# A two-stage convolution joint kernel: the second batch's first convolution as triples with running sums in one PSUM bank

## The chip, the cores and the metric

The kernel runs on one core of a Trainium2 chip. The metric is the device time of one launch in microseconds, the median of three runs. A core has five engines with queues of their own: TensorE (PE in the profile; it loads weights, PEld, and multiplies), VectorE (DVE), ScalarE (ACT), GpSimd (POOL) and SyncE (SP), which here only issues DMAs. TensorE writes its sums to PSUM, eight banks of 512 fp32 values in each of 128 partitions; VectorE and ScalarE read and write PSUM and SBUF, GpSimd SBUF alone.

## What is computed

```python
B, T, D, K, U = 2, 4000, 512, 5, 8       # x [B,T,D], w1, w2 [K,D,D], g [B,U,D], w_f, w_g, w_o [D,D], all bf16
xp = jnp.pad(x, ((0,0),(2,2),(0,0)))
h = sum(jnp.einsum("btc,cd->btd", xp[:, i:i+T, :], w1[i]) for i in range(K))
h = gelu(h)[:, ::2, :]                   # 2000 rows
hp = jnp.pad(h, ((0,0),(2,2),(0,0)))
f = sum(jnp.einsum("btc,cd->btd", hp[:, i:i+2000, :], w2[i]) for i in range(K))
f = gelu(f)[:, ::2, :]                   # 1000 rows: the features
fe = f @ w_f
ge = g @ w_g
j = jnp.tanh(fe[:, :, None, :] + ge[:, None, :, :])
return jnp.einsum("btud,dv->btuv", j, w_o)          # [2, 1000, 8, 512]
```

Two convolutions of five taps and stride two, each with a GELU, then a product with w_f, a tanh of its sum with each of 8 vectors, and a product with w_o for 16,000 rows.

## The kernel before

**Layout.** Channels lie on the 128 partitions, in four blocks (`NK`); time runs along the free dimension. The input is loaded by transposing DMAs, one for each phase of the row number, so that a stride becomes an offset. A "product" is one 512x128 weight matrix times one operand, for one block `m` of 128 outputs: four matmuls into one PSUM region.

**The first convolution, pairs from four phases.** `Tile_` makes outputs in pairs: from four phases of the input (rows modulo 4), with sums and differences of the phases and of the five weight matrices, two outputs cost 7 products where the plain way costs 10. `xf` (VectorE) makes the operands, `shift` (ScalarE) copies a phase moved by one. The first batch is cut into tiles of 252, 252 and 498 columns (tiles 0 to 2), the second into 504 and 498 (tiles 3 and 4). `unit(m)` runs the three products of the middle, a copy on ScalarE (`cs`), two VectorE sums back into PSUM, then (`end`) the four other products on top of these and a GELU to `hT`. `hT[b]` holds the result in six planes, by output number modulo 6.

**The second convolution, triples from six phases.** `Triple` makes three outputs with 9 products where the plain way costs 15. `HOME` says where each of the nine operands lies: in `row[b]` (place 0) or, in place, in `hT[b]` (place 1). `step` makes them: "2d" doubles three planes (two ScalarE copies, 1344 and 2688 values per partition), "r" takes their differences (VectorE, 4032), "prev" and "next" are copies of one plane on ScalarE, and nine further steps are VectorE operations of 1336. `unit(m)` uses three banks: t1 and s1 into b1, tm and sm into bm, t2 into b2; a ScalarE copy of b1; five VectorE operations of 334, two of which write back into PSUM; then t0 and s0 on top of b2, ti and si on top of bm. One output leaves from SBUF (`y`), two from PSUM, by GELU into `fT[b]` with a stride of three values (`o::3`). `w2part` makes the weight combinations.

**Features and outputs.** `fe(b)` multiplies the features by w_f; `ge` does g by w_g; `wosums` prepares sums of w_o on GpSimd in the place of w_g; `tanh(v, k)` on ScalarE writes a ring `jT`; `Plain` and `Seven` make the 125 output blocks of 128 rows, and `store` writes them to DRAM, with a cut wherever a block crosses from one of the 16 (batch, u) pairs to the next.

**Order.** The kernel is written as a list of operations. `Plan.edges` derives the dependences from SBUF bytes and PSUM banks, `Plan.schedule` fixes the order on each engine with a cost for each operation (0.16 us for a hand-over), and `emit` sets the semaphores. After line 823 the order on an engine isn't that of the list: TensorE, SP and GpSimd take the earliest entry of the list that is ready, ScalarE and VectorE the most urgent one. That order is fixed when the kernel is built; on the chip each engine goes strictly through its own.

**Names and lines of the change.** `load_x` (L417) with the calls in L441 to L442; `w2part` (L537); `Triple` (L639 to L732); `load_rest` (L839), which reloads `xs[0]` for the second batch and then loads w2 and the other weights; `tiles` and `trip` (L748 to L750); the tables `SUMS` and `LATE` (L897 to L904), which say after which unit each preparation is listed; the loops that follow; `store` (L957).

Of the kernel before, what the change touches and what calls it, by code (L numbers as in the profile page):

```python
# [12 lines left out]
P = 128  # L13
# [260 lines left out]
def bass_standalone__seq2seq_rnn_t_joint__speech_kernel(  # L274
# [36 lines left out]
    with ExitStack() as es:  # L311
# [22 lines left out]
        assert hT[0].end <= h_off + 16384 and xr[1].end <= cur[0]  # L334
        cs = [at(f"cs{i}", [NT], FP32) for i in range(2)]
# [10 lines left out]
        sd = [Buf(nc, f"sd{i}", [3, 336], FP32, s_off + i * 4096) for i in range(2)]  # L346
        assert sd[1].end <= ws[2].end
# [56 lines left out]
        for i in (0, 2):  # L404
            for ph in (2, 3):
                memset(xs[i][ph, :, 15:16])
# [17 lines left out]

        came = [load_xr(rt) for rt in range(2)]
# [15 lines left out]
        for ph in (2, 3, 1, 0):  # L441
            load_x(2, ph, 16, 528)  # L442
# [94 lines left out]
        def w2part(m, part):  # L537
# [7 lines left out]
            elif part == "p":  # L545
                stt("dve", w2_t[1, :, sl], w(2), 2.0, u)
                tt("dve", w(2), t, w(2), add)
            elif part == "a":
                act(w2_t[0, :, sl], v, ACT.Copy, scale=1.0 / 3.0)
                act(w(0), w(0), ACT.Copy, scale=0.5)  # L550
            else:
                sl = slice(m * P, (m + 2) * P)
                tt("dve", w2_t[2, :, sl], w2_sb[1, :, sl], w2_sb[3, :, sl], add)
                tt("dve", w2_t[3, :, sl], w2_sb[1, :, sl], w2_sb[3, :, sl], sub)
# [84 lines left out]
        class Triple:  # L639
# [5 lines left out]
            def __init__(self, b):  # L645
                self.b, self.z_, self.r_ = b, hT[b], row[b]

            def z(self, i, d=0, n=NT3):
                return self.z_[i, :, HOFF + d:HOFF + d + n]
# [4 lines left out]
            def step(self, which):  # L654
# [11 lines left out]
                elif which == "t2":  # L666
                    tt("dve", z(4), z(4), z(0), sub)
                elif which == "t1":
                    tt("dve", r(4), r(1), r(2), add)
                elif which == "tm":  # L670
                    tt("dve", r(5), r(2), r(1), sub)
                elif which == "ti":
                    tt("dve", r(3), r(1), r(3), sub)
                elif which == "t0":
                    tt("dve", r(0), r(0), r(2), sub)
                elif which == "s1":
                    tt("dve", z(0), z(1), z(3), add)
                elif which == "s0":
                    tt("dve", z(2), z(2), z(3), sub)
# [495 lines left out]
```

## Time and profile before

| | us |
|---|---|
| median of three runs (265.00 to 266.12) | 265.52 |
| the profiled execution | 265.86 |
| its span, first to last instruction | 264.1 |

The difference of some 1.8 us between the execution and its span lies around the span. The mean granted TensorE clock is 1.000.

Busy time by stage (us from the start of the span, busy us of each engine):

| stretch | what TensorE does | PE | DVE | ACT | POOL |
|---|---|---|---|---|---|
| 34.20 to 51.00 | first convolution, batch 0, tile 2 | 16.80 | 16.80 | 12.63 | 0.00 |
| 51.00 to 58.60 | tile 2 ends, tile 3 begins | 7.60 | 3.70 | 3.06 | 0.00 |
| 58.60 to 74.20 | tile 3 (batch 1) | 15.60 | 14.27 | 9.27 | 0.17 |
| 74.20 to 98.75 | tile 4 (batch 1) | 24.55 | 23.89 | 15.47 | 5.99 |
| 98.75 to 108.30 | tile 4 ends, second convolution begins | 9.55 | 4.44 | 3.22 | 0.00 |
| 108.30 to 131.60 | second convolution | 23.30 | 17.90 | 17.18 | 0.17 |
| 131.60 to 148.50 | features of batch 0, second convolution | 16.90 | 9.55 | 14.73 | 2.71 |
| 148.50 to 164.00 | second convolution ends, features of batch 1 | 15.35 | 7.38 | 11.66 | 11.04 |
| 164.00 to 264.00 | outputs | 96.10 | 85.72 | 89.28 | 58.74 |

A row of the timeline gives the start, the duration, engine, line, operation, output and input, shapes and count; rows of equal instructions are merged. The duration of one instruction reaches past the start of the next on the same engine, so what an instruction costs in a row of its kind is read from start to start. Nearly all operations are issued by helpers, so their line is that of the helper (L391 a matmul, L378 a tensor_tensor, L533 a scalar_tensor_tensor, L383 an activation) and the names of the operands tell them apart.

### The profile page before, as it was taken

The numbers are of one execution on the slowest core, as the hardware profiler recorded it, in microseconds if no ns is written. First come the engines' busy times: TensorE is split into PE (matmuls) and PEld (weight loads), VectorE is DVE, ScalarE is ACT, GpSimd is POOL, SyncE is SP. The second block draws the span as 40 slices with busy tenths as digits, with TensorE's granted clock in tenths as the row PEclk, the third lists the DMA queues.
The fourth block names the chain that finished last, engine by engine and source line by source line (L and its number), as shares of the span: only waits on it lengthen the run. The fifth ranks groups of instructions, "written<-read, shape, count | busy, mean of one in ns | idle before, by whom it ended". The sixth has DMA issues, their size and how long they took to land.

```text
span 264.1 us, 4770 instructions
## 1 busy us (share of the span) xinstructions
PE 257.3 (97%) x1738; PEld 167.3 (63%) x1738; DVE 209.9 (79%) x320; ACT 196.2 (74%) x269; POOL 80.1 (30%) x85
## 2 busy tenths in 40 slices
PE   8899999999999999999999999999999999999993
PEld 4797954444444445566646665777777777777782
DVE  1898999929999996299663744789899899889993
ACT  2637989348348723685679993898999999999942
POOL 1000000000000710000000974055785886929760
PEclk9999999999999999999999999999999999999999
DMA  6999999997000000000000000354454554645555
GB/s 246 301 178 196 201 211 217 191 352 224 2 0 0 0 2 0 0 2 1 0 2 0 20 24 0 126 167 159 155 185 142 170 180 139 207 144 171 168 181 172
DMA packets 54725, 31.92 MB, mean 121 GB/s; under 512 B 31646, under 2 KB 54446, under 8 KB 54702
## 3 DMA queue, kind: packets, MB, share of 16 engines
q1 hardware_dynamic: 54558, 31.55, 44.6%
q8 instruction: 14, 0.23, 0.4%
q14 instruction: 9, 0.07, 0.1%
q10 hardware_dynamic: 144, 0.07, 0.1%
HBM read 7.86 MB, written 16.38 MB: 92 GB/s over the span
## 4 chain that ended last, share of the span: by engine, by line
PE 88%; ACT 8%; DVE 1%; issue 1%; ACTq 0%
PE acc L391 88%; ACT jT L383 4%; ACT fT L383 2%; DVE xs L466 0%; ACT cs L383 0%; ACT xt L383 0%; ACT feT L383 0%; DVE xt L378 0%; DVE feT L872 0%; ACT og L383 0%; ACT hT L383 0%; PE acc L459 0%; ACTq L965 0%; ACT ost L383 0%; DVE zero L398 0%
## 5 line engine op out<-in xcount | busy, mean ns | idle before, releaser
L383 ACT ACTIVATE jT<-feT,geT 128x1000 bf16<-128x1000 f32 (+10 forms) x84 | 78.4, 1012 | 2.4 <-PE acc L391 1.4
L391 PE MATMUL acc<-wo_sb,jT 128*128 128x512 bf16 (+1 forms) x336 | 61.3, 323 | 0.0
L378 DVE TENSOR_TENSOR og<-acc,sn 128x512 bf16<-128x512 f32 x63 | 42.3, 684 | 9.9 <-ACT sn L383 7.4
L391 PE MATMUL acc<-xt,w_sb 128*128 128x252 bf16 (+2 forms) x240 | 45.9, 333 | 0.3 <-ACT hT L383 0.3
L378 POOL TENSOR_TENSOR ss<-jT 128x512 f16<-128x512 bf16 x21 | 24.4, 1164 | 71.5 <-PE acc L391 49.5
L391 PEld LDWEIGHTS acc<-wo_sb,jT 128*128 128x128 bf16 x336 | 32.9, 98 | 16.5
L383 ACT ACTIVATE sn<-acc 128x512 f32<-128x512 f32 x63 | 39.6, 677 | 4.3 <-PE acc L391 4.1
L391 PE MATMUL acc<-tw,ss 128*128 128x256 f16 x252 | 34.7, 273 | 0.0
L391 PEld LDWEIGHTS acc<-xt,w_sb 128*128 128x128 bf16 x240 | 23.3, 98 | 17.9 <-DVE ty L533 0.5
L955 DVE CAST ost<-acc 128x512 bf16<-128x512 f32 (+1 forms) x41 | 27.7, 676 | 2.4 <-PE acc L391 2.1
L391 PE MATMUL acc<-xs,w_t 128*128 128x498 bf16 (+2 forms) x140 | 29.5, 341 | 0.0
L391 PEld LDWEIGHTS acc<-tw,ss 128*128 128x128 f16 x252 | 24.6, 98 | 7.2
L383 ACT ACTIVATE hT<-acc 128x996 bf16<-128x996 f32 (+2 forms) x13 | 12.6, 968 | 21.0 <-PE acc L391 21.0
L378 POOL TENSOR_TENSOR ss<-jT,ss 128x512 f16<-128x512 bf16 x21 | 24.7, 1180 | 0.7
L378 POOL TENSOR_TENSOR ss<-ss,jT 128x512 f16<-128x512 f16 x21 | 24.5, 1169 | 0.7
L383 ACT ACTIVATE xt<-xs 128x1992 bf16<-128x1992 bf16 (+2 forms) x14 | 21.6, 1576 | 2.6 <-DMA xs<-in_x_dram 2.6
L391 PEld LDWEIGHTS acc<-xs,w_t 128*128 128x128 bf16 x140 | 13.5, 98 | 10.9 <-issue 0.3
L391 PE MATMUL acc<-xs,w_sb 128*128 128x252 bf16 (+2 forms) x104 | 19.3, 318 | 1.2 <-DVE xt L378 1.2
L378 DVE TENSOR_TENSOR ss<-jT 128x512 f16<-128x512 bf16 x21 | 16.7, 797 | 4.2 <-PE acc L391 2.2
L378 DVE TENSOR_TENSOR xt<-xt,xs 128x1992 bf16<-128x1992 bf16 (+2 forms) x14 | 14.2, 1012 | 5.7 <-ACT xt L383 5.7
L533 DVE SCALAR_TENSOR_TENSOR sd<-acc,cs 128x334 f32<-128x334 f32 x16 | 7.4, 499 | 12.9 <-PE acc L391 12.4
L391 PE MATMUL acc<-row,w_sb 128*128 128x334 bf16 x96 | 17.5, 305 | 0.0
(71 smaller groups left out, 363.3 us busy)
## 6 DMA issues: line engine op xcount, KB each, us to landing
out_dram<-og SPq DMA_DIRECT2D x75, 128.0 KB, 2.0
w_sb<-in_w_dram SPq DMA_DIRECT2D x10, 512.0 KB, 5.6
out_dram<-ost SPq DMA_DIRECT2D x34, 128.0 KB, 2.0
xr<-in_x_dram SPq DMA_DIRECT2D x2, 512.0 KB, 3.6
wg_sb<-in_w_g_dram SPq DMA_DIRECT2D x1, 512.0 KB, 8.8
wf_sb<-in_w_f_dram SPq DMA_DIRECT2D x1, 512.0 KB, 7.0
wo_sb<-in_w_o_dram SPq DMA_DIRECT2D x1, 512.0 KB, 7.9
xs<-in_x_dram SPq DMA_TRANSPOSE x16, 5.6
```

Of the source, the lines that this page charges most:

```text
L378: pl.op(eng, lambda e: e.tensor_tensor(out=o.ap, in0=a.ap, in1=b.ap, op=op), (a, b), (o,), 0.15 + 2.2e-3 * o.ap.free_size() if eng == "poo ...
L383: pl.op("act", lambda e: e.activation(o.ap, i.ap, func, scale=scale, bias=0.0 if bias is None else bias.ap), rd, (o,), o.ap.free_size() * ...
L391: ins = e.matmul(o.ap, lhsT=l.ap, rhs=r.ap, start=start and n == 0, stop=stop and n == len(pairs) - 1, skip_group_check=not check)
L533: pl.op(eng, lambda e: e.scalar_tensor_tensor(out=o.ap, in0=a.ap, scalar=f, in1=b.ap, op0=ALU.mult, op1=add), (a, b), (o,), vec_cost(o, (a ...
L955: pl.op("dve", lambda e: e.tensor_copy(out=o.ap, in_=v.ap), (v,), (o,), vec_cost(o, (v,)))
```

## The change

- **Input.** The second batch is loaded in six phases (rows modulo 6), 336 columns each, into `xp[2]` and, after the first batch's tile 1 is done, `xp[0]`, which lie in the place of `xs[2]` and `xs[0]`. For the last column of `xp[0]` four small DMAs load one row each, value by value.
- **First convolution of the second batch.** Tiles 3 and 4 go. Two `Triple`s (of 334 columns) take their place, with operands in `xp` and `row`, weights in `w1_sb`, `w1_t` and a new `w1_x`, and output to `hT[1]`.
- **Weights.** `w1part` makes w1's combinations while tile 2 runs, some in place in `w1_sb`, two of each block's sums on GpSimd. `w2part` scales some weights otherwise and moves the sum and difference of taps 1 and 3 to GpSimd, in blocks of 128. `w1_x` lies where w_f, w_g and w_o are kept, so these three are loaded later (`load_late`).
- **Units.** A unit of a triple uses one bank A for a running sum: t1 and s1, then ScalarE's copy `c`; tm and sm on top, then ScalarE's copy `s` (times -1.5); t2 on top, then two VectorE operations: `v` = A + s, and bank B = 2A + s. GpSimd adds `v` to `c`, from which one output leaves. t0 and s0 go on top of A, ti and si on top of B. The 16 units (two triples of the first convolution, two of the second, four blocks each, numbered 0 to 15) go through one loop in which three units overlap: s1 of t, s3 of t-1, s5 of t-2, s2 of t, s4 of t-1. `fixed` lists the preparation after each.
- **Features.** `fT` is written without a stride: outputs 0, 3, 6, ... first, then 1, 4, ..., then 2, 5, .... The rows of an output block are then three apart in DRAM, and `store` also cuts at the borders of these three planes (`R0`).

Kernel lines of the change, without the memory layout and the parts of `Triple.step` that are only rewritten:

```diff
+        xp = {i: Buf(nc, f"xp{i}", [6, NK, 352], BF16, xs[i].end - xs[i].bytes) for i in (0, 2)}
+        w1_x = Buf(nc, "w1_x", [3, NK, D], BF16, wf_sb.end - wf_sb.bytes)
...
+        def load_x6(i, b, ph, j0, col):
+            r0 = b * T + 6 * j0 + ph
+            dst = xp[i][ph, :, col:col + 336]
+            src = x.rearrange("b t d -> (b t) d")[r0:r0 + 6 * 335 + 1:6, :]
+            pl.dma("sp", lambda e: e.dma_start_transpose(out=dst.ap, in_=src), (), (dst,))
...
-        for ph in (2, 3, 1, 0):
-            load_x(2, ph, 16, 528)
+        for ph in (4, 0, 2, 1, 3, 5):
+            load_x6(2, 1, ph, 0, 16)
...
+                stt("dve", u, w(2), 2.0, u)
                 tt("dve", w(2), t, w(2), add)
-            elif part == "a":
                 act(w2_t[0, :, sl], v, ACT.Copy, scale=1.0 / 3.0)
-                act(w(0), w(0), ACT.Copy, scale=0.5)
+                act(w2_t[1, :, sl], u, ACT.Copy, scale=1.0 / 3.0)
             else:
-                sl = slice(m * P, (m + 2) * P)
-                tt("dve", w2_t[2, :, sl], w2_sb[1, :, sl], w2_sb[3, :, sl], add)
-                tt("dve", w2_t[3, :, sl], w2_sb[1, :, sl], w2_sb[3, :, sl], sub)
+                tt("pool", w2_t[2, :, sl], w(1), w(3), add)
+                tt("pool", w2_t[3, :, sl], w(1), w(3), sub)
+                act(w(1), w(1), ACT.Copy, scale=2.0)
+
+        def w1part(m, part):
+            sl = slice(m * P, (m + 1) * P)
+            w = lambda i: w1_sb[i, :, sl]
+            v, u = ssum[0][:], ssum[1][:]
+            if part == "s":
+                s = ws[m][:] if m < 2 else ws[2][:, (m - 2) * P:(m - 1) * P]
+                tt("dve", v, s, w(2), sub)
+                stt("dve", u, w(4), 4.0, w(0))
+                stt("dve", u, w(2), 2.0, u)
+                act(w1_x[0, :, sl], v, ACT.Copy, scale=1.0 / 3.0)
+                act(w1_x[1, :, sl], u, ACT.Copy, scale=1.0 / 3.0)
+                tt("pool", w(2), w(1), w(3), add)
+                tt("pool", w1_x[2, :, sl], w(1), w(3), sub)
+            else:
+                act(w(1), w(1), ACT.Copy, scale=2.0)
...
+            def s1(self):
+                self.A = banks.pop(0)
+                self.t.product("t1", self.m, self.A, True)
+                self.t.product("s1", self.m, self.A, False)
+                act(self.c, self.pa(), ACT.Copy)
+
+            def s2(self):
+                self.t.product("tm", self.m, self.A, False)
+                self.t.product("sm", self.m, self.A, False)
+                act(self.s, self.pa(), ACT.Copy, scale=-1.5)
+
+            def s3(self):
+                self.t.product("t2", self.m, self.A, False)
+                self.B = banks.pop(0)
+                tt("dve", self.v, self.pa(), self.s, add)
+                stt("dve", self.pb(), self.pa(), 2.0, self.s)
+                tt("pool", self.c, self.c, self.v, add)
+                self.t.out(1, self.m, self.c)
+
+            def s4(self):
+                self.t.product("t0", self.m, self.A, False)
+                self.t.product("s0", self.m, self.A, False)
+                self.t.out(0, self.m, self.pa())
+                banks.append(self.A)
+
+            def s5(self):
+                self.t.product("ti", self.m, self.B, False)
+                self.t.product("si", self.m, self.B, False)
+                self.t.out(2, self.m, self.pb())
+                banks.append(self.B)
...
+            for ph in (4, 0, 2, 1, 3, 5):
+                load_x6(0, 1, ph, 330, 0)
+            for ph in range(4):
+                d = xp[0][ph, :, 336:337]
+                pl.dma("sp", lambda e, d=d, ph=ph: e.dma_start(
+                    d.ap, x[1, T - 4 + ph:T - 3 + ph, :].rearrange("r (k p) -> p k r", p=P), allow_slow_non_contiguous=True), (), (d,), nbytes=65536)
             for i in (0, 1, 3, 4, 2):
                 load_w("sp", w2_sb[i], w2[i].rearrange("(k c) d -> c k d", c=P))
...
+        when(1, lambda: w1part(2, "d"), lambda: w1part(3, "d"), lambda: tail_zero(0))
+        steps(1, 1, 0, 4)
+        steps(2, 1, 4, 8)
+        steps(3, 1, 8, 13)
+        for m in range(NK):
+            when(1 + m, lambda m=m: w2part(m, "s"))
+            when(2 + m, lambda m=m: w2part(m, "d"))
+        steps(5, 2, 0, 4)
+        steps(6, 2, 4, 8)
+        steps(7, 2, 8, 13)
+        when(9, load_late, lambda: tail_zero(1))
+        steps(10, 3, 0, 4)
+        steps(11, 3, 4, 13)
+        when(12, ge)
+        when(13, lambda: fe(0))
+        when(14, lambda: tanh(0, 0), lambda: tanh(0, 1))
+        when(15, lambda: tanh(0, 2), lambda: tanh(0, 3))
+        nu = len(units)
+        for t in range(nu):
+            units[t].s1()
+            if t:
+                units[t - 1].s3()
+            if t > 1:
+                units[t - 2].s5()
+            else:
+                finish(1 - t)
+            units[t].s2()
+            if t:
+                units[t - 1].s4()
+            for f in fixed.get(t, ()):
+                f()
...
-                n = min((vv + 1) * T2, c0 + P) - lo
-                b, u, t = vv // U, vv % U, lo % T2
+                r = sum(lo % T2 >= q for q in R0[1:3])
+                n = min(vv * T2 + R0[r + 1], c0 + P) - lo
+                b, u, t = vv // U, vv % U, 3 * (lo % T2 - R0[r]) + r
                 s = src(lo - c0, lo - c0 + n)
-                dst = out[b, t:t + n, u, cl]
+                dst = out[b, t:t + 3 * n - 2:3, u, cl]
...
```

## The prediction

> **What bounds the kernel now.** I read the head of the page first, then what TensorE waits for, then its timeline for the price of a product, then VectorE's and GpSimd's timelines around the stages that change.
>
> The head of the page, and the rows of the span in 40 slices of 6.6 us:
> ```profile
> span 264.1 us, 4770 instructions
> PE 257.3 (97%) x1738; PEld 167.3 (63%) x1738; DVE 209.9 (79%) x320; ACT 196.2 (74%) x269; POOL 80.1 (30%) x85
> ...
> PE   8899999999999999999999999999999999999993
> ...
> DVE  1898999929999996299663744789899899889993
> ACT  2637989348348723685679993898999999999942
> POOL 1000000000000710000000974055785886929760
> ```
> PE is full in every slice between start and tail, at full granted clock. DVE is at 90% or more from slice 9 to 14 too (59 to 99 us), which is where the second batch's first convolution runs.
>
> All that TensorE waits for:
> ```profile
> PE acc L391 <- DVE zero L398: 1.2, 1, 1.2
> PE acc L391 <- DVE xt L378: 1.2, 1, 1.2
> PE acc L391 <- ACT hT L383: 0.3, 1, 0.3
> PE acc L391 <- DVE og L378: 0.2, 1, 0.2
> PE acc L391 <- ACT fT L383: 0.2, 1, 0.2
> ```
> 3.1 us in all, 2.4 of it before 9 us. So the time is the sum of matmul columns, and a product less is time gained as long as nobody else becomes late.
>
> TensorE's timeline, four matmuls (one product for one block of 128 outputs) to a row; the first number is the start:
> ```profile
> 68.80 1.01 PE L391 MATMUL acc<-xs,w_t 128*128 128x504 bf16 x4
> 69.64 1.01 PE L391 MATMUL acc<-xt,w_t 128*128 128x504 bf16 x4
> ...
> 86.99 1.00 PE L391 MATMUL acc<-xs,w_t 128*128 128x498 bf16 x4
> 87.83 1.00 PE L391 MATMUL acc<-xt,w_t 128*128 128x498 bf16 x4
> ...
> 98.75 0.73 PE L391 MATMUL acc<-row,w_sb 128*128 128x334 bf16 x4
> 99.31 0.73 PE L391 MATMUL acc<-hT,w_t 128*128 128x334 bf16 x4
> ```
> Durations overlap; the price is from start to start: 0.85 us for 504 columns (two such steps take 1.70), 0.84 for 498, 0.567 for 334 (98.75 to 100.45 is three).
>
> VectorE and then GpSimd around 90 us:
> ```profile
> 88.80 1.76 DVE L378 TENSOR_TENSOR hT<-hT 128x1336 bf16<-128x1336 bf16 x1
> 90.48 1.80 DVE L378 TENSOR_TENSOR row<-row 128x1336 bf16<-128x1336 bf16 x1
> ...
> 98.15 0.84 DVE L378 TENSOR_TENSOR hT<-hT 128x1336 bf16<-128x1336 bf16 x1
> 98.91 0.84 DVE L378 TENSOR_TENSOR row<-row 128x1336 bf16<-128x1336 bf16 x1
> ```
> ```profile
> 87.22 2.62 POOL L378 TENSOR_TENSOR tw<-wo_sb 128x512 f16<-128x512 bf16 x2 [24.45 <-PE acc L391]
> 89.80 3.49 POOL L378 TENSOR_TENSOR tw<-wo_sb,tw 128x512 f16<-128x512 bf16 x2
> ```
> The same step of a triple takes 0.76 us from start to start alone and 1.68 to 1.72 beside GpSimd. About 2.8 us were lost in three steps over 4.5 us of GpSimd (88.8 to 93.3): 0.63 us per us of overlap. The change puts GpSimd to work where it was idle, so this row matters most.
>
> **What it removes and adds on TensorE.** Removed: tiles 3 and 4, each 7 products x 4 blocks: 28 x 0.85 + 28 x 0.84 = 47.32 us. Added: two triples of 9 products x 4 blocks: 72 x 0.567 = 40.80. The second convolution keeps its 72 products, the features, sums and outputs their matmuls. Gain on the path: **6.52 us**, if TensorE stays full.
>
> **VectorE**, the cover that could break. Prices from start to start: first difference of a triple ("r") 2.18 us (85.45 to 87.63), its nine other steps 0.76 each, so 9.0 per triple; a weight sum of 512 0.60 (69.03 to 69.63); a sum on PSUM of 334 0.42, of 498 0.585 (two in 96.22 to 97.39). From 34.2 us (tile 2's first product) to unit 12's first (the second triple-batch of the second convolution) TensorE has 28 x 0.84 + 101 x 0.567 = 80.8 us: 12 units of nine products, less the seven of units 10 and 11 that come after it. In that time VectorE must do: what is left over from the tiles before (6.3, the rows from 34.6 to 42.5 that aren't tile 3's), tile 2's eight sums 4.7, four triples 36.1 less six steps that unit 12 needs later (4.6), w1's 12 weight sums 7.2, w2's 20 12.0, eleven units at two sums (five before) 9.2. Sum 70.9 of 80.8, so it fits with 10 us to spare.
>
> GpSimd alongside: 16 weight sums and 11 adds. A weight sum lies between 1.16 us (alone) and 1.74 (beside VectorE, the second pair above); I take 1.4. The fp32 add of 334 has no row; by elements it is 0.76 to 1.14, I take 0.95. Together 33 us, 41% of the stretch. VectorE's bf16 steps are the 36 us of triples; by chance 14.7 us of them lie beside GpSimd: 14.7 x 0.63 = 9.2 us. Bounds: 0 (all beside PSUM sums) and 33 x 0.63 = 20.8 (all beside steps). I take 9.2, as neither engine's order follows the other's: 80.1 of 80.8. VectorE thus goes from covered to just full.
>
> The Trainium skill ("GPSIMD Engine Reference", 1. Specifications) says more than the row: GpSimd shares its SBUF interfaces with VectorE, and every VectorE instruction with two SBUF inputs contends. The trace agrees for bf16 steps (1.68 against 0.76); no run here shows it for the weight sums, which also have two. By that rule 19.2 us more would be hit, 19.2 x 0.41 x 0.63 = 5.0 us, and VectorE would be 4.3 us over its stretch, for a time near 265.5.
>
> **ScalarE.** Per unit, two copies from PSUM of 334 (0.34 each, start to start, 0.45 long) and three GELUs (0.34 to 0.6); 6.0 us of copies per triple (3.55 for the pair of doublings, 81.77 to 85.32, then 1.2 twice); 24 weight scalings at 0.52 (86.68 to 87.20). With tile 2 and what is left before it 68 of 80.8 us, against 49.6 busy in that stretch now. It fits. Each unit adds two waits to TensorE: the next product into the same bank waits for ScalarE's snapshot. Behind the first lie three products of older units (1.70 us), behind the second four: a snapshot needs 0.45 plus about 0.1 of hand-over (0.02 to 0.14 in the chain of waits), so it is hidden. If it sits behind a 2.4 us doubling it costs 2.4 + 0.55 - 1.70 = 1.2 us; there are four such doublings, one per triple. The plan may run other units' products meanwhile.
>
> **Handovers.** Unit 12 needs hT[1] whole: unit 7's last product ends after 79 products, 57.7 + 44.8 = 102.5 us, GELU to 103.1, doublings 3.55, 0.5 of hand-over (the idle row before "r" says 0.62), "r" 2.18, three steps 2.3: 111.7, against a due time of 115.0. Three units' PSUM sums (2.5) and a unit of ScalarE (1.8) in between make it 116.0; all four VectorE pieces contended (4.5 more) 120.5, which is 5.5 late. TensorE has seven older products (4.0 us) to fill this. Units 4 and 8 have 3 to 4 us more room.
>
> **DMA.** Six transposes of 336 rows move what four of 512 did, at about 2.4 us per 512 KB one after the other. The one-column loads are 4 x 512 runs of two bytes; page section 3 gives 44.6% of 16 x 264 us over 54558 packets, 35 ns each, so 1.1 us per load on 16 engines, 4.5 together. They stand on SP ahead of w2, which then lands near 62 us; its sums can wait until 94. The last weights move behind unit 7's last use, three loads that land 7 to 9 us after issue, needed 12 us later. If this cover were gone, w2 late by x would be x on unit 8. On SP nothing stands behind the late loads until the first store at about 150. With w_o late, GpSimd's four sums of it (6.1 us, 87.2 to 93.3) move behind unit 12; their first product is at 155.26, so they stay hidden. I cost all at nothing. The split stores add about 32 issues at 0.45 us, 14 us, on SP, which waits for producers in every row of its list in the last 100 us: nothing. Contiguous feature writes make 24 GELUs shorter (0.74 towards 0.45 us), off the path where TensorE is full.
>
> **Sum.** Gain 6.52; loss between 0 and the 4.4 that handover and snapshots leave between them when some filler fails; I take the middle, 2.2. The profiled execution took 265.86 us: 265.86 - 6.52 + 2.2 = 261.5. The median is 0.34 lower: **261.2 us**; its own range, losses 0 to 4.2, is 259.0 to 263.2.
>
> **Rivals.**
> 1. *A late handover* (unit 12, with snapshots behind doublings). For: its chain has 3.3 us of slack alone, none contended. Against: the filler of 4.0 us, and 6.7 us of features that can run there. Without filler 5.5: 259.0 + 5.5 = 264.5 us.
> 2. *VectorE beside GpSimd becomes the bound.* Place: 34 to 115 us. Price 0.63 us per us of overlap. Without other loss it eats the gain when VectorE's work is 80.8 + 6.5 = 87.3, at 16.4 us of contention or 26 us of overlap out of 33; at all of it, 91.7, TensorE waits 10.9: 259.0 + 10.9 = 269.9 us. From 17.7 us of contention on it is slower beyond what can be told. For: the row, and adds that follow VectorE's sums at once, so they meet its next step. Against: half of VectorE's work is not bf16 steps.
> 3. *All hidden*: 259.0 us, a little less if the shorter GELUs help where the chain of waits runs through ScalarE (136 to 156 us).
>
> **Chances.** Forecast 0.56; late handover, 263.2 to 265.5, 0.17, half of it faster; contention, above 265.5, 0.24, 0.05 of it no change; all hidden and below 259.0, 0.03. A difference under 0.5% (1.33 us) can't be told from none here, so faster ends at 264.2 and slower begins at 266.85: 0.67, 0.14, 0.19. The range goes from 258.6 to 266.6 and leaves 0.2 out.
>
> **What would show it.** TensorE's 334-column products at 0.567 and 144 of them in triples; PE idle in 34 to 120 us of 0 to 4 us in all, its waits naming VectorE's hT or row at units 4, 8, 12; VectorE at over 95% busy there, with 1336-wide steps spread between 0.84 and 1.8; GpSimd about 33 us there. Wrong: over 5 us of PE waits on ScalarE's snapshots, or on a DMA; or VectorE with idle time while PE is full, so that contention was overrated.

## The result, and the profile after

The changed kernel takes **292.74 us** (median of four, 291.48 to 293.52) against 265.77 us in the same set of runs: a ratio of 1.101 [1.097, 1.106]. Predicted were 261.2 us and at most 266.6. The profiled execution took 292.66 us, its span 290.4, which is 26.3 us more than the 264.1 before. As the gain of 6.5 us was to come off, some 33 us were lost on the way.

The head of the page after, and the 40 slices, each now 7.3 us:
```profile
span 290.4 us, 5024 instructions
...
PE 259.2 (89%) x1788; PEld 172.9 (60%) x1802; DVE 215.2 (74%) x312; ACT 209.1 (72%) x319; POOL 124.6 (43%) x117
...
PE   8987999959985979899999999999978899985792
...
DVE  1999999953599999939622465787749798592982
...
POOL 1530200172476621121521794353953866298150
PEclk9999999996999799999999999999999999999999
```
Where TensorE was full in nearly every slice it now has holes in three places (slices counted from 0): shallow ones in slices 2 and 3, ahead of tile 2; deep ones between slices 8 and 14 (58 to 109 us), with reduced clock in slices 9 and 13, just after the deepest; and slices 29 to 37, in the outputs. GpSimd, which before did next to nothing until 86 us, works from slice 1 on.

All that TensorE waits for, the largest groups (us in total, times, longest):
```profile
PE acc L396 <- DVE acc L545: 6.7, 3, 3.3
PE acc L396 <- DVE og L383: 6.5, 6, 2.4
PE acc L396 <- DVE ost L1008: 3.3, 2, 2.7
PE acc L396 <- ACT sd L388: 2.7, 3, 1.7
PE acc L396 <- POOL w_sb L383: 1.7, 1, 1.7
PE acc L396 <- DVE w_t L383: 1.6, 3, 0.5
```
Three of these are in the units of the triples (`acc` written by VectorE, `sd` by ScalarE, `w_sb` by GpSimd), two in the outputs (`og`, `ost`), and `w_t` lies before tile 2, in the weights of the first batch.

Three marks divide the span, and they are used for every run below: tile 2's first product, the first product of the features of batch 1, and the end.

| us | before tile 2 | tile 2 to features of batch 1 | from there to the end |
|---|---|---|---|
| before | 34.2 | 122.2 | 107.7 |
| after | 37.9 | 132.8 | 119.7 |
| difference | +3.7 | +10.6 | +12.0 |

The middle should have become 6.5 us shorter, so 17.1 us are lost there. The last part, which the prediction costed at nothing, lost 12.0 us on its own.

### The profile page after: what moved, and what is told of

The parts are those of the page before. It is cut to its first block, busy times and chain, and to the rows that moved or that the text cites. A ratio compares the mean times of both kernels' runs of the same rounds, so it can differ in the third digit from the quotient of the medians.

```text
span 290.4 us, 5024 instructions
## 1 busy us (share of the span) xinstructions
PE 259.2 (89%) x1788; PEld 172.9 (60%) x1802; DVE 215.2 (74%) x312; ACT 209.1 (72%) x319; POOL 124.6 (43%) x117
## 4 chain that ended last, share of the span: by engine, by line
PE 49%; DVE 21%; DMA 8%; issue 6%; ACT 6%; SPq 5%; POOL 2%; ACTq 0%; DVEq 0%
PE acc L396 49%; DMA out_dram<-ost 8%; SPq L1019 5%; DVE row L383 4%; DVE xt L383 2%; DVE acc L545 2%; ACT jT L388 2%; POOL w_sb L383 2%; DVE xp L383 2%; DVE og L383 2%; DVE w_t L383 2%; ACT sn L388 1%; DVE ws L383 1%; DVE ws L545 1%; DVE ssum L383 1%
## 5 line engine op out<-in xcount | busy, mean ns | idle before, releaser
L396 PE MATMUL acc<-wo_sb,jT 128*128 128x256 bf16 (+1 forms) x322 | 60.1, 321 | 4.0 <-DVE ost L1008 3.3
L396 PEld LDWEIGHTS acc<-wo_sb,jT 128*128 128x128 bf16 x336 | 32.7, 98 | 20.1 <-DVE ost L1008 3.8
L383 POOL TENSOR_TENSOR sd<-sd 128x334 f32<-128x334 f32 x16 | 14.5, 905 | 58.3 <-DVE sd L383 51.4
L396 PE MATMUL acc<-row,w_sb 128*128 128x334 bf16 x160 | 29.4, 306 | 6.7 <-DVE acc L545 6.7
L396 PE MATMUL acc<-tw,ss 128*128 128x256 f16 x252 | 34.7, 273 | 0.0
L396 PE MATMUL acc<-xt,w_sb 128*128 128x252 bf16 (+1 forms) x144 | 25.1, 319 | 0.9 <-DVE xt L383 0.9
L396 PEld LDWEIGHTS acc<-row,w_sb 128*128 128x128 bf16 x160 | 15.1, 98 | 15.6 <-DVE acc L545 8.4
L383 POOL TENSOR_TENSOR w_sb<-w_sb 128x512 bf16<-128x512 bf16 x4 | 10.2, 2554 | 32.7 <-DVE ssum L545 19.5
L396 PE MATMUL acc<-xp,w_sb 128*128 128x334 bf16 x96 | 18.0, 312 | 1.7 <-POOL w_sb L383 1.7
L396 PE MATMUL acc<-tw,jT 128*128 128x256 f16 x84 | 12.7, 273 | 6.5 <-DVE og L383 6.5
L388 ACT ACTIVATE sd<-acc 128x334 f32<-128x334 f32 x32 | 14.3, 446 | 4.2 <-PE acc L396 4.1
L383 DVE TENSOR_TENSOR row<-row 128x1336 bf16<-128x1336 bf16 x16 | 16.9, 1054 | 0.0
```

The costliest lines, as they stand in the source:

```text
L383: pl.op(eng, lambda e: e.tensor_tensor(out=o.ap, in0=a.ap, in1=b.ap, op=op), (a, b), (o,), 0.15 + 2.2e-3 * o.ap.free_size() if eng == "poo ...
L388: pl.op("act", lambda e: e.activation(o.ap, i.ap, func, scale=scale, bias=0.0 if bias is None else bias.ap), rd, (o,), o.ap.free_size() * ...
L396: ins = e.matmul(o.ap, lhsT=l.ap, rhs=r.ap, start=start and n == 0, stop=stop and n == len(pairs) - 1, skip_group_check=not check)
```

## The experiments

All ratios are to the kernel before, run on the same chip in the same set.

### The outputs in the order of time again

The features get their old stride and the stores their old cuts; everything else stays as in the changed kernel.
```diff
-                act(fT[b][m, R0[r]:R0[r + 1]], src.map(lambda a: a[:, 0:n]), ACT.Gelu_apprx_tanh, scale=1.0 if r else 0.5)
+                act(fT[b][m, r::3], src.map(lambda a: a[:, 0:n]), ACT.Gelu_apprx_tanh, scale=1.0 if r else 0.5)
...
-                r = sum(lo % T2 >= q for q in R0[1:3])
-                n = min(vv * T2 + R0[r + 1], c0 + P) - lo
-                b, u, t = vv // U, vv % U, 3 * (lo % T2 - R0[r]) + r
+                n = min((vv + 1) * T2, c0 + P) - lo
+                b, u, t = vv // U, vv % U, lo % T2
...
-                dst = out[b, t:t + 3 * n - 2:3, u, cl]
+                dst = out[b, t:t + n, u, cl]
```


> The changed kernel with its features in time order again: GELUs write with a stride of three, a store is cut only where (batch, u) changes. From the features of batch 1 to the end the changed kernel took 119.7 us of its span, the one before 107.65. Theory: the stores of the planes cost these 12 us, so 280 to 282 us. Rival: the outputs are late because ScalarE and GpSimd reach them late; then the stores are a symptom and the time stays within 3 us of 292.7.

282.26 us, 1.061 [1.056, 1.065]: 10.5 us less than the changed kernel. The outputs take 108.0 us, as before the change. So the layout by planes costs the outputs their 12 us; the rest of the loss stands. The whole gains less than 12 us, as the middle becomes 1.8 us longer, 134.6 against 132.8; a GELU to `fT` takes 0.74 us there with the stride of three, and 0.46 without.

### That layout alone, in the kernel before

```diff
-                n = (T2 - o + 2) // 3
-                act(fT[self.b][m, o::3], src.map(lambda a: a[:, 0:n]), ACT.Gelu_apprx_tanh)
+                R0 = (0, 334, 667, 1000)
+                n = R0[o + 1] - R0[o]
+                act(fT[self.b][m, R0[o]:R0[o + 1]], src.map(lambda a: a[:, 0:n]), ACT.Gelu_apprx_tanh)
...
-                n = min((vv + 1) * T2, c0 + P) - lo
-                b, u, t = vv // U, vv % U, lo % T2
+                R0 = (0, 334, 667, 1000)
+                r = sum(lo % T2 >= q for q in R0[1:3])
+                n = min(vv * T2 + R0[r + 1], c0 + P) - lo
+                b, u, t = vv // U, vv % U, 3 * (lo % T2 - R0[r]) + r
...
-                dst = out[b, t:t + n, u, cl]
+                dst = out[b, t:t + 3 * n - 2:3, u, cl]
```


> The kernel before, with only the features by output plane and the stores that follow from it. Theory: the stores alone cost about 12 us, 276 to 279 us. Rival (outputs were late for another reason): 265 to 267 us, or a little under, since the 24 GELUs get shorter.

277.73 us, 1.047 [1.043, 1.051]; the outputs take 119.8 us. The layout does this without any triple in the first convolution. It consists of three things: contiguous features, rows three apart in DRAM, and cuts at 334 and 667. The next two runs take the cuts alone.

### The cuts alone, at 334 and 667, and at 336 and 672

Both keep the kernel before and the order of time, and only cut the stores more often.
```diff
-                n = min((vv + 1) * T2, c0 + P) - lo
+                R0 = (0, 334, 667, 1000)
+                n = min(vv * T2 + next(q for q in R0 if q > lo % T2), c0 + P) - lo
```


> The kernel before, features in time order, rows next to each other in DRAM, but every run of rows cut also at 334 and 667 of each 1000, as the planes cut it (172 stores in place of 140). Theory of the uneven cuts (odd row counts go to few DMA engines): nearly all of the 12 us, 275 to 279 us. Rival of the stride (rows three apart): 265 to 268 us. Theory of the issues: also 275 to 279, told apart by the next run.

```diff
-                n = min((vv + 1) * T2, c0 + P) - lo
+                R0 = (0, 336, 672, 1000)
+                n = min(vv * T2 + next(q for q in R0 if q > lo % T2), c0 + P) - lo
```


> As the run with cuts at 334 and 667, but cut at 336 and 672: about as many stores, every one a multiple of 8 rows. Theory of the uneven cuts: 265 to 268 us. Theory of the issues on SP: 274 to 279 us.

The cuts at 334 and 667, 172 stores: 278.15 us, 1.047 [1.044, 1.050]. The cuts at 336 and 672, 170 stores, each a multiple of 8 rows: 266.90 us, 1.003 [1.001, 1.005]. So the 30 further issues cost about 1 us. The other 11 us come with cuts that lie two to five rows elsewhere: the pieces then have uneven numbers of rows (61, 107, 109), where the even cuts leave multiples of 8. No cost of the rows three apart is seen: the plain cuts give the same time as the layout within the two intervals.

The stores of `og` in the trace. First SP's issues of them in the changed kernel (ns of one issue: least, median, most), and from issue to landing:
```profile
L1019 SPq DMA_DIRECT2D out_dram<-og x116: 255/401/3520, 180.3 to 286.8; - x116
...
DMA to landing us min/median/max: 1.7/3.7/6.8
```
The same of the kernel before with even cuts:
```profile
L966 SPq DMA_DIRECT2D out_dram<-og x114: 292/414/1426, 165.7 to 261.7; - x114
...
DMA to landing us min/median/max: 1.7/2.0/2.7
```
And of the kernel before with the cuts at 334 and 667:
```profile
L966 SPq DMA_DIRECT2D out_dram<-og x116: 260/393/3187, 165.9 to 275.2; - x116
...
DMA to landing us min/median/max: 1.9/3.4/6.7
```
The number of issues and their median are nearly the same in all three. What differs is how long a store takes to land (2.0 us against 3.4 to 3.7 in the median, up to 6.8), and that single issues stretch from 0.4 to over 3 us. The uncut kernel has 1.7/2.0/2.6. These landings are only those that the profile can assign: with the cuts at 334 and 667 they are 14 stores, all of them whole blocks of 128 rows. So the line shows that even a whole store lands late there, among the uneven ones; it does not show the uneven ones themselves.

A few pieces of the chain that ended last, in the changed kernel (start, us, what):
```profile
214.45 3.94 DMA out_dram<-ost
218.39 0.60 DVE ost L1008
...
220.71 3.74 DMA out_dram<-ost
...
225.10 3.80 DMA out_dram<-ost
```
A store must land before its buffer can be written again (`ost` by VectorE). Where a landing takes nearly 4 us, VectorE waits for the buffer, TensorE then for VectorE to empty PSUM: the 9.8 us of waits for `og` and `ost` above.

The Trainium skill ("DMA: Bandwidth & Descriptors", in the section on why a DMA increments its semaphore by 16) says that the queue takes for each transfer the largest number of engines up to 16 that divides the slowest dimension of both sides. An estimate by that rule: before the change all 140 stores go to 8 to 16 engines; with cuts at 334 and 667, 39 of the 172, with 2637 of the 16,000 rows, go to fewer than 8, and 12 of them to a single one. The trace agrees: on each of the 15 semaphores of the stores, before and after the change and with either set of cuts, the number of updates that come from the DMAs is what the rule gives, 16 for a store on 16 engines and one more than the rule's number for every other. With these numbers the updates of every block of 128 rows can be told apart. In the changed kernel the ten blocks with a piece on a single engine landed 6.5 us after their last issue in the median and 10.1 at most, and the 85 blocks wholly on 16 engines 4.3 us, against 2.0 before.

### The same stores, cut into multiples of 16 rows and a rest

The changed kernel with planes, where each run of rows is split so that its first part is a multiple of 16.
```diff
                 n = min(vv * T2 + R0[r + 1], c0 + P) - lo
+                n = n - n % 16 or n
```


> The changed kernel, planes kept, but every run of rows is cut into a multiple of 16 rows and a rest of under 16. Theory of the uneven cuts: a run of 37 or 67 rows can't be shared out over many DMA engines, so with cuts at 16 most of the 12 us come back, 281 to 285 us. Rival of the stride: rows that lie three apart in DRAM are slow, whatever the cut, 291 to 294. Rival of the issues: SP issues too many stores; some 40 more make it 295 or more.

293.58 us, 1.105 [1.100, 1.109]: no better. The landings are short again (1.7, 1.8 and at most 3.8 us), but there are 242 stores instead of 172, and at 0.42 us each they take 100 us of SP's time in outputs of 122 us. TensorE still waits 6.7 us for VectorE's `og`. It looks as if one fault had been exchanged for another, but that the issues on SP are the limit here was not tested; the fault of uneven rows is shown by the pair of runs before this, not by this one.

### The 16 weight sums on VectorE instead of GpSimd

In the changed kernel, with planes:
```diff
-                tt("pool", w2_t[2, :, sl], w(1), w(3), add)
-                tt("pool", w2_t[3, :, sl], w(1), w(3), sub)
+                tt("dve", w2_t[2, :, sl], w(1), w(3), add)
+                tt("dve", w2_t[3, :, sl], w(1), w(3), sub)
...
-                tt("pool", w(2), w(1), w(3), add)
-                tt("pool", w1_x[2, :, sl], w(1), w(3), sub)
+                tt("dve", w(2), w(1), w(3), add)
+                tt("dve", w1_x[2, :, sl], w(1), w(3), sub)
```


> The changed kernel with the 16 sums and differences of taps 1 and 3 of both weights on VectorE, not on GpSimd; the 16 adds of units stay there. Theory: they cost VectorE more from GpSimd (31.4 us of GpSimd, each VectorE operation beside it about 1 us longer) than on itself (16 x 0.35 = 5.6 us); the 3.7 us lost before tile 2 come back and most of the 17 us of waits between tile 2 and the features of batch 1, so 272 to 280 us. Rival: VectorE was full already, the sums push it over; 293 to 298 us.

276.99 us, 1.043 [1.039, 1.047]: 15.7 us less than the changed kernel, although VectorE gets 16 instructions more. They take 0.33 us each there from start to start where nothing hinders them, 5.3 us for 16, and are busy for 7.5 us in the trace; on GpSimd the same sums took 31.4 us. The marks are 34.7 and 154.5, so start and middle gain 3.2 and 13.0 us.

What the sums did on GpSimd is seen from 85 to 99 us in the changed kernel. VectorE's timeline there:
```profile
85.98 1.80 DVE L383 TENSOR_TENSOR row<-row 128x1336 bf16<-128x1336 bf16 x1
87.70 1.80 DVE L383 TENSOR_TENSOR xp<-xp 128x1336 bf16<-128x1336 bf16 x1
...
91.15 0.84 DVE L383 TENSOR_TENSOR xp<-xp 128x1336 bf16<-128x1336 bf16 x1
...
94.61 1.64 DVE L545 SCALAR_TENSOR_TENSOR ws<-w_sb 128x512 f32<-128x512 bf16 x1
96.17 1.64 DVE L383 TENSOR_TENSOR ssum<-ssum,w_sb 128x512 f32<-128x512 f32 x1
```
GpSimd's, three sums to a row:
```profile
85.30 5.21 POOL L383 TENSOR_TENSOR w_t<-w_sb 128x512 bf16<-128x512 bf16 x3
...
94.10 4.72 POOL L383 TENSOR_TENSOR w_t<-w_sb 128x512 bf16<-128x512 bf16 x3
```
And TensorE's:
```profile
89.56 0.74 PE L396 MATMUL acc<-xp,w_x 128*128 128x334 bf16 x4
93.65 0.74 PE L396 MATMUL acc<-row,w_sb 128*128 128x334 bf16 x4 [3.35 <-DVE acc L545]
94.23 0.73 PE L396 MATMUL acc<-xp,w_sb 128*128 128x334 bf16 x4
94.79 1.20 PE L396 MATMUL acc<-row,w_t 128*128 128x334 bf16 x4
95.79 1.32 PE L396 MATMUL acc<-xp,w_sb 128*128 128x334 bf16 x4
```
Beside GpSimd (85.3 to 90.5) a step of a triple takes 1.72 us from start to start, alone (91.15) 0.76; and a weight sum of 512, 0.60 us alone, takes 1.56. So the weight sums are slowed as the steps are. VectorE has no idle time here; its units' sums on PSUM come after the steps, and TensorE waits 3.35 us for them.

The Trainium skill ("GPSIMD Engine Reference", 1. Specifications) says that every VectorE instruction with two inputs from SBUF contends with GpSimd. The weight sums at 1.56 against 0.60 us show it here.

The loss is not only VectorE's pace. Around 60 us the chain goes through four engines. In the changed kernel GpSimd, then ScalarE, then VectorE:
```profile
56.93 6.90 POOL L383 TENSOR_TENSOR w_sb<-w_sb 128x512 bf16<-128x512 bf16 x2 [18.91 <-DVE ssum L545]
```
```profile
62.76 0.63 ACT L388 ACTIVATE w_sb<-w_sb 128x512 bf16<-128x512 bf16 x1 [5.24 <-POOL w_sb L383]
```
```profile
64.83 0.69 DVE L383 TENSOR_TENSOR ssum<-ws,w_sb 128x512 f32<-128x512 f32 x1 [3.11 <-ACT w_x L388]
```
The first row is two sums; the second of them, and VectorE's steps beside the first:
```profile
62.69 1.15 POOL L383 TENSOR_TENSOR w_sb<-w_sb 128x512 bf16<-128x512 bf16 x1
```
```profile
56.78 0.84 DVE L383 TENSOR_TENSOR xp<-xp 128x1336 bf16<-128x1336 bf16 x1
57.54 0.84 DVE L383 TENSOR_TENSOR row<-row 128x1336 bf16<-128x1336 bf16 x1
```
So the first sum took 5.8 us (56.93 to 62.7) and the second 1.15. VectorE's steps beside the first kept their usual 0.76 us: here GpSimd bore the whole contention. Behind the first sum stands a scaling in ScalarE's fixed order (5.24 us idle), behind that the scalings that free `ssum` for VectorE (3.11 us idle), and TensorE waits 1.7 us for the sum and 1.7 for ScalarE's snapshot.

### Sums on GpSimd in the kernel before

Of the change, only w2's sums of taps 1 and 3 move to GpSimd, in blocks of 128 (eight instructions of 512 instead of four of 1024 on VectorE).
```diff
-                sl = slice(m * P, (m + 2) * P)
-                tt("dve", w2_t[2, :, sl], w2_sb[1, :, sl], w2_sb[3, :, sl], add)
-                tt("dve", w2_t[3, :, sl], w2_sb[1, :, sl], w2_sb[3, :, sl], sub)
+                for i in (m, m + 1):
+                    sl = slice(i * P, (i + 1) * P)
+                    tt("pool", w2_t[2, :, sl], w2_sb[1, :, sl], w2_sb[3, :, sl], add)
+                    tt("pool", w2_t[3, :, sl], w2_sb[1, :, sl], w2_sb[3, :, sl], sub)
```


> The kernel before, with one part of the change alone: the sum and the difference of w2's taps 1 and 3 on GpSimd, eight operations of 512 in place of four of 1024 on VectorE. Theory: VectorE is full from 59 to 99 us; it saves 4 x 0.60 = 2.4 us and loses about 1 us beside each GpSimd sum, 8 in all, so TensorE waits 2 to 6 us, 268 to 272 us. Rival: VectorE gains 2.4 us and the time stays at 265 to 266.5.

269.56 us, 1.014 [1.011, 1.016]: 3.4 us slower, though VectorE has less to do. Six of the sums took 9.9 us, 1.65 each. The prediction's rate of 0.63 us lost per us of overlap would make that 6.2 us of VectorE's time. TensorE, full before, shows one wait of 2.94 us that ends at 89.2 us, and half a clock after it for 1.7 us more; its middle is 4.8 us longer than before (127.0 against 122.2). The wait is for ScalarE's GELU to `hT`, which stands behind two doublings (84.6 to 88.2 us) and these behind a scaling that waited 1.7 us for VectorE's `ssum`. So the loss came as a late link in ScalarE's order, 15 us after the last of the moved sums. The orders on the engines moved with the edit, so not all of the 3.4 us is shown to be contention.

### Time order and sums on VectorE together

The changed kernel with the first edit above and the sums' one, whose cores are:
```diff
-                act(fT[b][m, R0[r]:R0[r + 1]], src.map(lambda a: a[:, 0:n]), ACT.Gelu_apprx_tanh, scale=1.0 if r else 0.5)
+                act(fT[b][m, r::3], src.map(lambda a: a[:, 0:n]), ACT.Gelu_apprx_tanh, scale=1.0 if r else 0.5)
...
-                tt("pool", w(2), w(1), w(3), add)
+                tt("dve", w(2), w(1), w(3), add)
...
```

> The changed kernel with both undone: features in time order, and the 16 weight sums on VectorE. If the two losses add up, 292.7 - 10.5 - 15.7 = 266.5; but the trace of dve_sums reaches the features of batch 1 at 154.5 us, 1.9 us ahead of the kernel before, and the outputs in time order took 108 us, so 262 to 265 us. A rival says that ScalarE, with strided GELUs again, becomes the bound: 267 to 270.

265.97 us, 0.9995 [0.998, 1.001]. The two costs lie in different stages and add up: 10.5 and 15.7 singly make 26.2, and together the two edits bring 26.8. The expectation of 262 to 265 had counted on the features of batch 1 at 154.5 us, as in the run before with contiguous writes; with the stride they come at 156.4. The kernel now stands where it stood before the change; the gain of 6.5 is still covered by something.

### The units' adds on VectorE too

On top of the last kernel, GpSimd's last part in the triples: the add of `v` to `c`, 16 instructions of 334.
```diff
-                tt("pool", self.c, self.c, self.v, add)
+                tt("dve", self.c, self.c, self.v, add)
```


> As order_dve, and the 16 adds of units on VectorE too, so that GpSimd has no sum in this stretch. Each add on GpSimd makes VectorE's next step 0.5 us longer (1.36 for 0.84 in dve_sums); on VectorE it costs 0.42. Theory: no dearer for VectorE and a hand-over less before the GELU, 0 to 2 us less than order_dve. Rival: VectorE's own 6.7 us more make it late, 1 to 4 us more than order_dve.

261.76 us, 0.984 [0.982, 0.986]: 4.2 us less, where 0 to 2 were expected. Windows of 20 us (start and end; length; busy us and instructions of PE, PEld, DVE, ACT, POOL; granted clock; DMA), with the adds on GpSimd:
```profile
75.00:95.00 20.00, 19.14 (x134) 12.75 (x133) 20.00 (x28) 13.47 (x27) 3.06 (x4) 1.00 0.00 1
95.00:115.00 20.00, 18.23 (x125) 11.52 (x124) 18.31 (x31) 14.13 (x26) 3.68 (x5) 1.00 0.26 80
```
and on VectorE:
```profile
75.00:95.00 20.00, 20.00 (x143) 13.72 (x142) 20.00 (x34) 13.65 (x28) 0.00 (x0) 1.00 0.00 1
95.00:115.00 20.00, 19.86 (x141) 13.41 (x140) 20.00 (x37) 16.36 (x29) 0.17 (x1) 1.00 0.25 80
```
In the first 20 us VectorE is full in both and does 28 instructions with GpSimd beside it, 34 without. Each add meets the step that follows the unit's sums, as these rows show, GpSimd's and VectorE's, of the run with planes, the sums on VectorE and the adds on GpSimd (step 1.28 us from start to start instead of 0.76):
```profile
74.04 0.89 POOL L383 TENSOR_TENSOR sd<-sd 128x334 f32<-128x334 f32 x1 [6.13 <-DVE sd L383]
```
```profile
74.28 1.36 DVE L383 TENSOR_TENSOR xp<-xp 128x1336 bf16<-128x1336 bf16 x1
75.56 0.84 DVE L383 TENSOR_TENSOR row<-row 128x1336 bf16<-128x1336 bf16 x1
```
The 0.5 us that an add costs VectorE is more than the 0.4 that it takes on VectorE, but 0.1 us for each of 16 adds is 1.6 us at most. TensorE's waits for `sd`, `acc` and `fT` fall from 3.8 to 0.9 us, which is most of the 4.2; that they fall because the unit's own chain has a hand-over less is argued, not shown.

### w1's weight work held back until tile 2

In the changed kernel, four of w1's sums are put on GpSimd at 10.4 us, among the first batch's weights: they were the earliest entries ready in the plan. Here every operation of `w1part` depends on tile 2's first product.
```diff
         def w1part(m, part):
+            first = len(pl.ops)
+            w1part_(m, part)
+            for o in pl.ops[first:]:
+                o.after.append(gate[0])
...
+        gate.append(len(pl.ops))
```


> The changed kernel with w1's weight work (on ScalarE, VectorE and GpSimd) held back until tile 2's first product. Theory: the four GpSimd sums at 10.4 to 16.7 us made VectorE's steps of tile 0 late, so tile 2 begins at 34 to 35 us in place of 37.9; the sums are still due later, where VectorE is full, so of these 3 us between 0 and 3 stay: 289.5 to 293. Rival: tile 2 begins late for another reason (loads, order), and its start stays at 37 to 38.

291.61 us, 1.096 [1.093, 1.099]: 1.1 us less, which the two intervals do not tell apart. What VectorE did at the start, in the kernel before and in the changed one:
```profile
11.26 1.22 DVE L378 TENSOR_TENSOR w_t<-w_sb 128x2048 bf16<-128x2048 bf16 x1
```
```profile
13.53 2.17 DVE L383 TENSOR_TENSOR w_t<-w_sb 128x2048 bf16<-128x2048 bf16 x1
```
Held back, the first stretch is 34.0 us long instead of 37.9, so the early weight work is what made it late; with the sums on VectorE it was 34.7, so nearly all of it was the sums on GpSimd. But the middle grows from 132.8 to 134.9 us, TensorE's waits for VectorE's `acc` from 6.7 to 8.7 and its wait for GpSimd's `w_sb` from 1.7 to 3.0: the sums now collide there.

### All three edits and the hold

The kernel of the adds (time order, sums and adds on VectorE) with the hold of `w1part`:
```diff
-                tt("pool", self.c, self.c, self.v, add)
+                tt("dve", self.c, self.c, self.v, add)
...
+            for o in pl.ops[first:]:
+                o.after.append(gate[0])
...
```

> As order_dve_adds (features in time order, weight sums and adds on VectorE), with w1's weight work held back until tile 2's first product. There TensorE waited 1.3 us for VectorE at 23.8 us, behind four early weight sums at 12.8, and tile 2 began at 35.2 (34.2 in the kernel before). Theory: 0.5 to 1.3 us less, 260.4 to 261.3. Rival: the work is missed later, 262 to 264.

**260.40 us**, 0.979 [0.977, 0.981]: the fastest, and the change's triples are all in it. The page's rows:
```profile
span 258.0 us, 4983 instructions
...
PE 251.3 (97%) x1802; PEld 173.1 (67%) x1802; DVE 216.5 (84%) x344; ACT 210.8 (82%) x319; POOL 79.5 (31%) x85
...
PE   8999999999999999999999899999999999999993
```
and its waits:
```profile
PE acc L396 <- DVE zero L403: 1.2, 1, 1.2
PE acc L396 <- ACT sd L388: 0.7, 1, 0.7
```
Parts of the span: 33.3, 117.1 and 107.6 us, against 34.2, 122.2 and 107.7 before. The median gains 5.8 of the 6.5 us. The middle, where the triples are, gains 5.1; the 0.9 us at the start lie within what the start varies by (33.25 to 34.2 in the kernel before and its variants).

### The largest doubling in two

The same, with "2d"'s copy of 2688 values split into two of 1344, since TensorE's wait for `sd` is for a snapshot queued behind it.
```diff
-                    act(r(slice(1, 3), n=E), z(slice(0, 4, 2), 0, E), ACT.Copy, scale=2.0)
+                    act(r(1, n=E), z(0, 0, E), ACT.Copy, scale=2.0)
+                    act(r(2, n=E), z(2, 0, E), ACT.Copy, scale=2.0)
```


> As best_gate, with the 2688-wide doubling on ScalarE cut into two of 1344, so that a snapshot waits behind 1.3 us and not 2.4. Snapshots behind a doubling cost TensorE 1.15 us once in dve_sums. Theory: 0 to 0.7 us less than best_gate. Rival: a fixed cost of 0.1 us for each of four more copies, no difference.

260.72 us, 0.980 [0.978, 0.982]; its wait for `sd` is 1.2 us in two places instead of 0.7 in one. No gain: the plan orders ScalarE anew, and another snapshot is late.

## Why the prediction was wrong

The sum of what was lost by place: 3.7 us before tile 2, 17.1 in the middle, 12.0 in the outputs, 32.8 in all; 265.9 - 6.5 + 32.8 = 292.2, against 292.66 of the profiled execution.

- **The gain on TensorE: right.** A product of 334 columns costs 0.57 us in the changed kernel too, and when little else is late (the best version) 5.8 of 6.52 us appear in the median, 5.1 of them in the middle.
- **"I cost all at nothing ... The split stores ... nothing": the step with the second largest error, 12.0 us.** It counted the issues and their time on SP, and there it was right: 30 more cost 1 us. It did not ask over how many engines a store of so many rows is spread, and so how long it and the stores around it take to land: 4.3 us in the median for the blocks wholly on 16 engines instead of 2.0, 6.5 us for those with a piece on one. The order of the rows in DRAM, which could have been suspected, costs nothing that is seen.
- **VectorE's budget without contention (70.9 of 80.8 us): about right.** With the 16 sums and the stretch's 11 adds as VectorE's own it becomes 70.9 + 16 x 0.33 + 11 x 0.4 = 80.6 of 80.8 us; without any of them on GpSimd VectorE is busy for 77.9 of the 81.0 us from 34 to 115, and TensorE has next to no gap there.
- **"By chance 14.7 us of them lie beside GpSimd: 14.7 x 0.63 = 9.2 us" and "VectorE thus goes from covered to just full": the step that failed most, 17.1 us in the middle.** The term itself was only somewhat small. From tile 2 to unit 12 GpSimd had 32.7 us of sums and adds, as predicted (33), though only 11 of the 16 sums fell there. Each VectorE instruction there, set against what its shape takes alone, adds up to an estimate of 13 us lost, some 5 of them in the weight sums that the prediction had set apart. That alone would have put VectorE about 3 us over its stretch. What failed is that GpSimd's work was priced only as lost pace of VectorE, averaged over the stretch. VectorE idled for 11 us between 61 and 76 us, waiting for ScalarE and then for TensorE, and was full from there to 118 us, where the sums of the units came late.
- **What follows a late sum: no term.** GpSimd's sums are links from which ScalarE and VectorE, in fixed orders, hang. One that took 5.8 us instead of 1.15 left them idle for 5.24 and 3.11 us, and cost TensorE 3.4 us of waits and 2.9 of clock around 62 us. VectorE's late sums cost 6.7 us of waits and 1.7 of clock between 84 and 105 us; two late snapshots cost 1.1. That is 15.8 of the 17.1 us.
- **The start, 3.7 us, in no term.** The prediction began its look at GpSimd at 34 us; the plan lets any entry that is ready run at once, and these were ready at 10 us.
- **The clock, about 4.6 us, in no term.** Its rows are in the last section.
- **The snapshots: right.** A snapshot behind a doubling was to cost 1.2 us; with the sums on VectorE it costs 1.15 us at one place (111.05 us). Five us of such waits would have been the sign against the forecast; 2.7 came.
- **Contiguous feature writes**: shorter GELUs on ScalarE as expected. The prediction put them off the path, but with the triples they are worth 1.5 to 1.8 us of the middle (119.8 against 121.3 us with the sums on VectorE, 132.8 against 134.6 with them on GpSimd). In the kernel before it is 0.3 (121.9 against 122.2).
- **The rivals.** The second, contention as the bound, is the mechanism of the middle. Its far end, 10.9 us of TensorE waits, was taken as a bound with little weight; the middle shows 11.1 us of waits (6.7, 2.7 and 1.7 above), and 4.6 of lost clock on top. That the two numbers are so close is luck: only the 6.7 are waits for VectorE. Late hand-over of unit 12 was not seen.

Left open: whether contiguous writes with stores cut at multiples of 8 would bring the best version the 1.5 us that they are worth above (it was not run), and how 1.4 us of the gain are lost in the middle of the best version, of which the waits name 0.7 as a snapshot.

## What to carry to other kernels

Work that is moved from a full engine to an idle one is not free when the two slow each other, as VectorE and GpSimd do here: price it as an overlap with whatever the full engine does at that time, on both sides, and look at what is queued behind its result on all other engines. When a transfer is cut, look at the number of rows of each piece as well as at the number of pieces. And when several changes come in one, each of them should be tried alone: here the triples gave most of what they were to give, and two side changes, a layout and a choice of engine, cost five times as much.

## What the runs showed of the hardware

**The clock falls after holes of under 3.4 us.** Windows of the changed kernel (as above; the clock is the number after POOL's):
```profile
62.00:66.00 4.00, 1.55 (x8) 0.74 (x9) 1.01 (x2) 3.24 (x7) 1.84 (x2) 0.77 0.04 13
66.00:71.00 5.00, 5.00 (x14) 1.95 (x13) 2.39 (x4) 3.26 (x5) 2.04 (x2) 0.50 0.00 0
90.00:95.00 5.00, 1.65 (x13) 0.94 (x11) 5.00 (x7) 1.02 (x2) 2.26 (x3) 0.99 0.00 0
95.00:98.50 3.50, 3.50 (x15) 1.92 (x14) 3.50 (x3) 1.93 (x4) 3.50 (x3) 0.53 0.00 0
```
The granted clock was 0.50 for 6.8 us after the first hole and for 3.4 us after the second: 4.87 us for 12 matmuls of 498 that cost 2.5 at the full clock, with the product before them 2.9 us lost; and three products in 3.2 us instead of 1.7, with the next 1.7 lost. No single wait was over 3.4 us; the first hole was two waits of 1.7 with one product between them. In the kernel before with sums on GpSimd a wait of 2.94 us was enough, and in the run with w1's work held back one of 2.14 us (half the clock from 84.5 to 87.9). A hole of this size need not do it: in the run with stores cut at 16 rows the same two waits of 1.7 us left the clock at 1.00 (62 to 71 us). The Trainium skill ("TensorE: Matmul & The Clock Gate", Part 1) puts the change at an idle window of about 3.4 us that runs freely. A free-running window fits with the same waits ending both ways; that it must be wholly idle does not fit with the first hole or with 2.14 us.

**Stores whose number of rows divides badly make the stores around them slow, and the issues too.** With 39 stores of 172 on fewer than 8 engines, blocks wholly on 16 engines land after 4.2 to 4.3 us in the median instead of 2.0, single issues on SP take up to 3.5 us, and the outputs lose 12 us.

**GpSimd is slowed by VectorE as VectorE is by GpSimd.** A sum of 512 takes 1.15 us alone, 1.6 to 5.8 beside VectorE, and 0.33 on VectorE itself. Which side loses differs: a step of 1336 takes 1.72 us instead of 0.76 at 86 us, and its usual 0.76 beside the sum of 5.8 us.
